# New step lengths and weights for the plan that orders a fused attention and feed-forward kernel

## The chip, the core and the metric

The kernel runs on one core of a Trainium2 chip. The core has a matrix engine (TensorE, in the profile PE for products and PEld for its weight loads), three engines for elementwise work (VectorE as DVE, ScalarE as ACT, GpSimd as POOL) and SyncE (SP), whose queue issues all transfers here. Each engine takes its own instructions in the order in which they were built; engines wait for one another through semaphores. PSUM is the memory into which TensorE writes; SBUF is the working memory.

The metric is the device time of one execution in microseconds (us), as the median of several runs. The profile is of one further execution.

## The reference, cut to what matters

```python
def mab(q, kv):
    s = scale * (q @ kv.transpose(0, 2, 1))
    s = s - s.max(-1, keepdims=True)
    a = np.exp(s)
    a /= a.sum(-1, keepdims=True) + 1e-09
    return a @ kv
h = mab(I, x)          # 32 inducing points attend to 12480 tokens of 128 numbers, 4 batches
attn = mab(x, h)       # every token attends to the 32 results

h = attn.reshape(-1, 128) @ w_in      # 128 x 2048
r = np.maximum(h, 0.0)
g = s * (r * r) + b
out = g @ w_out                       # 2048 x 128
```

All of it is float32, for 49920 tokens.

## The kernel before

**Tiles.** The tokens go in blocks of 480 (BLK), 26 to a batch, 104 in all. The hidden size of 2048 is cut into 16 columns of 128, taken two at a time: a *pair* k is two such columns for one block, a tile of 128 partitions x 2 x 480. There are 8 pairs to a block and 832 in all. `pair(k)` (L813) makes one of them.

**A pair.** PE multiplies the block's attention weights with a matrix in which the attention's result and w_in are joined (L824, two products, into one of three PSUM buffers h). Then r = relu(h) goes to SBUF, by ACT (L840) or by DVE (L842), as the plan chooses. ACT squares r into g1 (`square`, L901), rounded to the narrower float fp32r; where two pairs of the same r tile are ready together, one instruction squares both (960 or 1920 columns). DVE forms the exact square relu(h) x r (L860), and the difference of that and g1, the low part g2, is formed at L878. PE then adds into the block's output bank x: g1 with the low and high parts of w_out, four products, and g2 with the high part, two products (`out_part`, L926). When a block is full, ACT (or DVE) scales it and adds the bias (L934, L936), and SP stores it.

**Two kinds of pair.** In a pair of kind P, DVE writes relu(h) x r to one of four SBUF buffers g, which frees the PSUM buffer h, and POOL subtracts. In a pair of kind D, DVE writes it in place into h and subtracts it itself; h stays taken until then. In the trace, L860 with g<-h,r is a P and L860 with h<-h,r is a D; L878 is on POOL or on DVE. The first 8 pairs (NATIVE) do without a low part, with one product of full float32 for each column.

**Beside the pairs** run the units of the attention: `attend` (L702 to L733) makes a block group's attention weights; `scores`, `top`, `values` and `points` (L614 to L689) prepare the next batch's 32 results, and `w_unit` (L564) the joined matrix. Each block's output bank alternates with one for these units. The first 60 us or so are an opening with the first batch's attention and the splitting of the weights.

**What sets the order.** Nothing on the chip chooses: the class Plan (L76) runs while the kernel is built, and records each instruction when its step is picked. A step is what a generator yields: an engine (or a choice of two) with a length in us, and events that must come first. Plan keeps a clock for each engine, and picks in turn the step that can start earliest, weighted by its urgency:

```python
at, eng = min(((max(ready, self.free.get(e, 0.0)), e) for e in engs),
              key=lambda x: x[0] + engs[x[1]] + lean.get(x[1], 0.0))
able.setdefault(eng, []).append((at + WEIGHT * urgency, at, engs[eng], u))
```

So the lengths decide where a step with a choice goes and who is first on an engine. LAT is the time that an event takes to be seen, SLIP how far another step may push the picked one back, LEAN and R_LEAN what is added for an engine where there is a choice (R_LEAN for r alone). M_U, R_U, S_U, C_U, SQ, OUT and OUT_HI are added to k as the urgency of the product, r, DVE's square, the in-place subtraction, ACT's square and the two output parts. MM is the length of one product. A pair becomes a P where POOL's planned backlog, `pool_work`, is under POOL_Q and a g buffer is free:

```python
wait = max(0.0, pool_work[0] - plan.end)
kind = "P" if wait < POOL_Q and next_free("g", 4) <= plan.start else "D"
```

The lengths and the constants work on the order alone: no instruction waits for a time on the chip.

Of the kernel before, what the change touches and what calls it, by code (L numbers as in the profile page):

```python
# [19 lines left out]
P = 128  # L20
# [5 lines left out]
TB = BLK // 32  # L26
TH = 8
WC = 512

POOL_Q = 4.228  # L30


LAT = 0.180
SLIP = 0.159
WEIGHT = 0.0272
LEAN = {"ACT": -0.50}
R_LEAN = {"DVE": 0.00}


M_U = -5.604  # L40
R_U = 2.437
SQ = 3.369
MM = 0.2165
S_U = -1.313
C_U = -5.000
OUT_HI = 1.632
OUT = 1.982
FRONT = 0.379
FIRST = -200.0
SPREAD = -50.0  # L50
# [3 lines left out]
NATIVE = 8  # L54
# [21 lines left out]
class Plan:  # L76
# [13 lines left out]
    def _step(self, unit, urgency, ready=None):  # L90
        want = next(unit, None)
        if ready is None:
            ready = self.end + LAT
        if want is not None:
            eng, us, *waits = want
            if not isinstance(eng, dict):
                engs, lean = {eng: us}, LEAN
            elif isinstance(us, dict):
# [20 lines left out]
    def run(self):  # L119
        ev = self.events  # L120
        while self.units:
            able = {}
            for u in self.units:
                _, urgency, ready, engs, waits, _, lean = u
                if any(w not in ev for w in waits):
                    continue
                ready = max([ready] + [ev[w] + LAT for w in waits])
                at, eng = min(
# [6 lines left out]
            for eng, steps in able.items():  # L135
                best = min(steps, key=lambda x: x[0])

                fill = [x for x in steps if x[1] + x[2] <= best[1] + SLIP]
                picks.append((*min(fill or [best], key=lambda x: x[0])[1:], eng))
# [8 lines left out]
def tile_attn_relu2(ctx: ExitStack, tc: tile.TileContext, xT, xN, indT, w_in, w_out, s_rep, b_rep, outT):  # L148
# [10 lines left out]
    plan = Plan()  # L159
# [71 lines left out]
    def blocks_in(g):  # L231
        return min(GR, NBLK - g * GR)
# [256 lines left out]
    def h_unit(b, ps, *waits):  # L489
# [17 lines left out]
        nc.vector.reduce_sum(out=l, in_=lw, axis=AX.X)  # L507
        plan.spawn(h_sums(b, l, lambda: ps), FIRST, plan.end + LAT)
        yield "DVE", 0.35
# [45 lines left out]
    def w_unit(b, ps, *waits):  # L555
# [19 lines left out]
        for c in range(nc_):  # L575
            plan.spawn(spread_w(b, c, hl, n, left), SPREAD + c, plan.end + LAT)

# [16 lines left out]
    def scores(b, g, ps, *waits):  # L594
        nb = blocks_in(g)
        rows = M * nb
        if g == 0:
            yield "DVE", 0.15, *waits
            d = st[b] = {
                "mx": sm.tile([P, NG], F32, name="mx"),  # L600
                "l": sm.tile([P, NG], F32, name="l"),
                "s": p1.tile([P, NG, BLK], F32, name="s"),
                "acc": sm.tile([P, P], F32, name="accb", bufs=1),
            }
            last = M * blocks_in(NG - 1)
            if last < P:
                nc.vector.memset(d["mx"][last:P, NG - 1:NG], -3.0e38)
                nc.vector.memset(d["l"][last:P, NG - 1:NG], 0.0)
        d = st[b]
        yield "PE", 0.4 + 0.23 * nb, ("x", b, g, 1), *waits  # L610
        ps = ps()
        xt, turn = xt_tiles[b, g, 1]
        for q in range(nb):
            nc.tensor.matmul(ps[M * q:M * (q + 1), 0:BLK], ind_sb, xt[:, q], start=True, stop=True)  # L614
        plan.set(("xt", turn))
        yield "DVE", 0.65
        nc.vector.reduce_max(out=d["mx"][0:rows, g:g + 1], in_=ps[0:rows, 0:BLK], axis=AX.X)
        yield dict(ACT=0.56, DVE=0.65), 0.0
        copy(d["s"][0:rows, g], ps[0:rows, 0:BLK])
        plan.set(("scores", b, g))  # L620
# [14 lines left out]
    def values(b, g, ps, *waits):  # L635
        d = st[b]
        rows = M * blocks_in(g)
        e = d["s"][0:rows, g]
        yield "ACT", 0.8, ("top", b), *waits
        nc.scalar.activation(  # L640
            out=e, in_=e, func=AF.Exp, bias=d["nm"][0:rows], scale=scale, accum_out=d["l"][0:rows, g:g + 1]
        )
        e_turn, e_free = ring_in_order("eT", 3)
        yield "DVE", 0.66, *e_free
        eT = sm.tile([P, TB, M], F32, name="eT", bufs=3)
        plan.set(("eT", "got", e_turn))
        nc.vector.transpose(out=eT[0:rows].rearrange("p n i -> p (n i)"), in_=e)  # L647
        yield "PE", 1.25, *[("xn", b, g, half) for half in range(-(-TB // TH))]
        ps = ps()
        for n in range(TB):  # L650
            c, half = n % (P // M), n // TH
            nc.tensor.matmul(  # L652
                ps[M * c:M * (c + 1), 0:P], eT[0:rows, n], xn_tiles[b, g, half][0][0:rows, n - half * TH],
                start=n < P // M, stop=n + P // M >= TB,
            )
        for half in range(-(-TB // TH)):
            plan.set(xn_tiles.pop((b, g, half))[1])
        plan.set(("eT", e_turn))
        yield "DVE", 0.29
        if g == 0:  # L660
            nc.vector.tensor_copy(out=d["acc"], in_=ps[:, 0:P])
        else:
            nc.vector.tensor_tensor(out=d["acc"], in0=ps[:, 0:P], in1=d["acc"], op=ALU.add)
        plan.set(("p1", b, g))
# [29 lines left out]
    def attend(b, g, ps, *waits):  # L694
        nb = blocks_in(g)
        rows = M * nb
        yield "PE", 0.4 + 0.23 * nb, ("hT", b), ("x", b, g, 2), *waits
        ps = ps()
        hT = st[b]["hT"]
        xt, turn = xt_tiles[b, g, 2]  # L700
        for q in range(nb):
            nc.tensor.matmul(ps[M * q:M * (q + 1), 0:BLK], hT[:, 0:M], xt[:, q], start=True, stop=True)  # L702
        plan.set(("xt", turn))
        s = ps[0:rows, 0:BLK]
        v = s.rearrange("p (n i) -> p n i", i=M)
        sums = ps[0:rows, BLK:BLK + TB]
        yield "DVE", 0.65
        nc.vector.transpose(out=s, in_=s)  # L708
        yield "DVE", 0.65
        mx = sm.tile([P, TB], F32, name="mx2")[0:rows]  # L710
        nc.vector.reduce_max(out=mx, in_=v, axis=AX.X)  # L711
        yield "DVE", 0.66
        nc.vector.tensor_tensor(out=v, in0=v, in1=mx.unsqueeze(2).broadcast_to([rows, TB, M]), op=ALU.subtract)
        yield "ACT", 0.55
        nc.scalar.activation(out=v, in_=v, func=AF.Exp, scale=scale)  # L715
        yield "DVE", 0.65
        nc.vector.reduce_sum(out=sums, in_=v, axis=AX.X)  # L717
        yield "DVE", 0.16
        nc.vector.tensor_scalar_add(sums, sums, 1e-9)
        yield "DVE", 0.17  # L720
        l = sm.tile([P, TB], F32, name="l2")[0:rows]
        nc.vector.reciprocal(out=l, in_=sums)
        yield "DVE", 0.66
        nc.vector.tensor_tensor(out=v, in0=v, in1=l.unsqueeze(2).broadcast_to([rows, TB, M]), op=ALU.mult)
        yield "DVE", 0.65
        nc.vector.transpose(out=s, in_=s)  # L726
        n, free = ring_in_order("hl", 2)
        yield dict(ACT=0.56, DVE=0.65), 0.0, *free
        hl = p2.tile([P, 2, WC], F32R, name="hl")[:, :, 0:BLK]
        plan.set(("hl", "got", n))  # L730
        copy(hl[0:rows, 0], s)
        yield "DVE", 0.66
        nc.vector.tensor_tensor(out=hl[0:rows, 1], in0=s, in1=hl[0:rows, 0].bitcast(F32), op=ALU.subtract)  # L733
        plan.set(("hl", b, g))
        mine = [q for q in range(nb) if (b, GR * g + q) not in a2t]
        halves[b, g] = hl, n, list(mine)
        for q in mine:
            plan.spawn(spread(b, g, q), SPREAD, plan.end + LAT)

# [71 lines left out]
    pool_work = [0.0]  # L811

    def pair(k):  # L813

        b, blk, pr = place(k)
# [14 lines left out]
        if n == 0:  # L830
            quad[k] = {"r": ring("r", 2), "g1": ring("g1", 4), "g1_uses": 4, "r_uses": 4, "R": []}
        q = quad[k - n]
        yield dict(ACT=0.855, DVE=1.08), R_LEAN, R_U, q["r"][1]
        if n == 0:
            q["r_t"] = ew.tile([P, 4, BLK], F32, name="r", bufs=2)
        native = k < NATIVE
        half = slice(2 * n, 2 * n + 2)
        r = q["r_t"][:, half, :]
        if plan.eng == "ACT":
            nc.scalar.activation(out=r, in_=hv, func=AF.Relu)  # L840
        else:
            nc.vector.tensor_scalar(out=r, in0=hv, scalar1=0.0, scalar2=None, op0=ALU.max)  # L842
        plan.set(("R", k))
        if native:
            g1_used(q, 2)
            q["r_uses"] -= 1
            kind = "N"
            g_turn, g_free = ring("g", 4)
            yield "DVE", 1.07, S_U, g_free
        else:  # L850
            q["R"].append((n, plan.end))
            if len(q["R"]) == 1:
                plan.spawn(square(k - n), k + SQ, plan.end + LAT)
            yield "DVE", 1.07, S_U
            wait = max(0.0, pool_work[0] - plan.end)
            kind = "P" if wait < POOL_Q and next_free("g", 4) <= plan.start else "D"
            if kind == "P":
                g_turn, _ = ring("g", 4)
        g = hv if kind == "D" else ew.tile([P, 2, BLK], F32, name="g", bufs=4)
# [9 lines left out]
            plan.spawn(out_part(k, ops, 1.6, "w_out", lambda: plan.set(("g", g_turn))), k + OUT, plan.end + LAT)  # L869
            return  # L870
        if kind == "P":
            pool_work[0] = max(pool_work[0], plan.end) + 2.17
        n2, free2 = ring("g2", 8)
        yield ("Pool", 2.17, ("Q", k), free2) if kind == "P" else ("DVE", 1.07, C_U, ("Q", k), free2)
        hi = q["g1_t"][:, half, :]
        g2 = ew.tile([P, 2, BLK], F32R, name="g2", bufs=8)
        eng = nc.gpsimd if kind == "P" else nc.vector
# [227 lines left out]
```

## Time and profile before

| | |
|---|---|
| median of 3 runs | 1641.07 us (1640.85 to 1641.46) |
| profiled execution, its own time | 1639.56 us |
| its span, first to last instruction | 1637.8 us |
| granted TensorE clock, mean | 0.997 |
| HBM read, written | 73.52 MB, 25.56 MB |
| transfers' share of 16 DMA engines | 24.3% |

The profile counts an engine as busy while one of its instructions runs. A group's row has its line, engine, operation, tiles (written <- read), shape and count, then busy time and mean ns of one, then the engine's idle time just before them and what ended most of it. Rows of a stretch have, for each engine in the order PE, PEld, DVE, ACT, POOL, busy time and (in brackets) instructions, then the granted clock, the DMA share and GB/s. Rows of the timeline have start, duration, engine, line, operation, tiles and count. Rows of waits have who waited for whom, with total us, times and the longest.

### The profile page before, as it was taken

Reading aid. Unit: us, or ns where it says so; the run is one execution under the profiler, and the core shown is the slowest. Engines: PE = TensorE matmul, PEld = TensorE weight load, DVE = VectorE, ACT = ScalarE, POOL = GpSimd, SP = SyncE. Lnnn points to the kernel's source line nnn. Section 1 sums busy time; section 2 is a strip of 40 time slices with the busy share of each in tenths; the row PEclk is TensorE's granted clock in tenths of the full one; section 3 lists DMA queues with packets and bytes.
Section 4 is the critical chain, followed back from the end, with each engine's and each line's share of the span. In section 5 each row is a group of like instructions: output and inputs, shape, how many; then the busy total and the mean of one; then the engine's idle time right before and its main releaser. Section 6 shows DMA issues by size and latency. Waiting matters only on the chain. (4 is left out here: it accounts for less than half of the span.)

```text
span 1637.8 us, 24676 instructions
## 1 busy us (share of the span) xinstructions
PE 1606.7 (98%) x8147; PEld 1288.9 (79%) x8147; DVE 1454.3 (89%) x1569; ACT 1500.6 (92%) x1755; POOL 1575.8 (96%) x718
## 2 busy tenths in 40 slices
PE   8899999999999999999999999999999999999998
PEld 6577788887887778887778777788778878888887
DVE  6989898989998889888988889989999899998996
ACT  7699999999998899998999999999989999999997
POOL 1499999999999999999999999999999999999998
PEclk9999999999999999999999999999999999999999
DMA  7332222312123222231222322322222112112110
GB/s 261 100 101 97 80 78 97 109 49 87 46 94 115 83 81 87 77 115 55 70 65 97 106 76 73 115 79 85 68 61 67 37 49 67 31 50 66 52 33 20
DMA packets 53982, 130.20 MB, mean 79 GB/s; under 512 B 11488, under 2 KB 37984, under 8 KB 53856
## 3 DMA queue, kind: packets, MB, share of 16 engines
q1 hardware_dynamic: 53856, 128.63, 24.3%
q8 instruction: 66, 1.08, 0.3%
q14 instruction: 60, 0.49, 0.1%
HBM read 73.52 MB, written 25.56 MB: 60 GB/s over the span
## 5 line engine op out<-in xcount | busy, mean ns | idle before, releaser
L878 POOL TENSOR_TENSOR g<-g,g 128x960 fp32r<-128x960 f32 x699 | 1558.8, 2533 | 13.9 <-DVE g L860 13.9
L926 PE MATMUL x<-g,w_hi 128*128 128x480 f32 x3296 | 1046.5, 382 | 5.1 <-POOL g L878 4.6
L860 DVE SCALAR_TENSOR_TENSOR g<-h,r 128x960 f32<-128x960 f32 x707 | 801.8, 1149 | 116.2 <-POOL g L878 61.3
L901 ACT ACTIVATE g<-r 128x960 fp32r<-128x960 f32 x808 | 797.8, 1020 | 40.1 <-DVE r L842 25.0
L926 PEld LDWEIGHTS x<-g,w_hi 128*128 128x128 f32 x3296 | 612.4, 188 | 131.5 <-POOL g L878 27.3
L840 ACT ACTIVATE r<-h 128x960 f32<-128x960 f32 x653 | 619.9, 967 | 56.4 <-PE h L824 49.4
L926 PE MATMUL x<-g,w_lo 128*128 128x480 f32 x1648 | 626.3, 380 | 0.0
L824 PE MATMUL h<-a2t,wst 128*128 128x480 f32 x1664 | 510.8, 388 | 11.2 <-DVE g L860 7.2
L824 PEld LDWEIGHTS h<-a2t,wst 128*128 128x128 f32 x1664 | 302.8, 189 | 105.8 <-issue 32.6
L926 PEld LDWEIGHTS x<-g,w_lo 128*128 128x128 f32 x1648 | 309.3, 188 | 51.7 <-issue 3.4
L842 DVE TENSOR_SCALAR r<-h 128x960 f32<-128x960 f32 x179 | 205.5, 1149 | 16.5 <-PE h L824 15.1
L878 DVE TENSOR_TENSOR g<-h,g 128x960 fp32r<-128x960 f32 x125 | 143.8, 1150 | 6.7 <-ACT g L901 1.4
L860 DVE SCALAR_TENSOR_TENSOR h<-h,r 128x960 f32<-128x960 f32 x125 | 144.6, 1157 | 2.6 <-ACT r L840 1.9
L934 ACT ACTIVATE ob<-x,bias,s_sb 128x480 f32<-128x480 f32 x103 | 77.1, 749 | 9.2 <-PE x L926 8.9
L316 POOL TENSOR_TENSOR w_in_sb<-w_in_sb,g 128x512 f32<-128x512 f32 x4 | 5.2, 1310 | 31.6 <-DVE g L311 31.6
L702 PE MATMUL x<-xt,hT 128*32 128x480 f32 x208 | 29.1, 594 | 0.0
L652 PE MATMUL x<-xn,eT 128*32 128x128 f32 (+1 forms) x630 | 22.5, 275 | 1.7 <-DVE eT L647 1.7
L652 PEld LDWEIGHTS x<-xn,eT 128*32 128x32 f32 (+1 forms) x630 | 16.9, 109 | 8.9 <-DVE eT L647 6.2
L733 DVE TENSOR_TENSOR hl<-x,hl 128x480 fp32r<-128x480 f32 (+1 forms) x28 | 18.2, 650 | 4.9 <-ACT hl L179 4.4
L614 PE MATMUL x<-xt,ind_sb 128*32 128x480 f32 x156 | 21.2, 578 | 0.0
L726 DVE STREAM_TRANSPOSE x<-x 128x480 f32<-128x480 f32 (+1 forms) x28 | 19.5, 697 | 1.0
L717 DVE TENSOR_REDUCE x<-x 128x15 f32<-128x480 f32 (+1 forms) x28 | 18.4, 656 | 2.2 <-ACT x L715 2.0
(151 smaller groups left out, 409.0 us busy)
## 6 DMA issues: line engine op xcount, KB each, us to landing
xt<-in_xT_dram SPq DMA_DIRECT2D x41, 960.0 KB, 5.2
out_dram<-ob SPq DMA_DIRECT2D x104, 240.0 KB, 2.0
a2t<-hl SPq DMA_DIRECT2D x412, 60.0 KB, 2.0
xn<-in_xN_dram SPq DMA_DIRECT2D x18, 512.0 KB, 3.6
xn<-in_xN_dram SPq DMA_DIRECT2D x18, 448.0 KB, 4.3
xt<-in_xT_dram SPq DMA_DIRECT2D x13, 480.0 KB, 4.1
wst<-hl SPq DMA_DIRECT2D x64, 64.0 KB, 2.0
r<-in_xT_dram SPq DMA_DIRECT2D x7, 480.0 KB, 9.0
```

The source lines that it names most:

```text
L614: nc.tensor.matmul(ps[M * q:M * (q + 1), 0:BLK], ind_sb, xt[:, q], start=True, stop=True)
L652: nc.tensor.matmul(ps[M * c:M * (c + 1), 0:P], eT[0:rows, n], xn_tiles[b, g, half][0][0:rows, n - half * TH], start=n < P // M, stop=n + P ...
L702: nc.tensor.matmul(ps[M * q:M * (q + 1), 0:BLK], hT[:, 0:M], xt[:, q], start=True, stop=True)
L726: nc.vector.transpose(out=s, in_=s)
L824: nc.tensor.matmul(h[:, u, 0:BLK], wst[:, c * P:(c + 1) * P], A, start=True, stop=True)
L840: nc.scalar.activation(out=r, in_=hv, func=AF.Relu)
L842: nc.vector.tensor_scalar(out=r, in0=hv, scalar1=0.0, scalar2=None, op0=ALU.max)
L860: nc.vector.scalar_tensor_tensor(out=g, in0=hv, scalar=0.0, in1=r, op0=ALU.max, op1=ALU.mult)
L878: eng.tensor_tensor(out=g2, in0=g, in1=hi.bitcast(F32), op=ALU.subtract)
L901: nc.scalar.activation(out=q["g1_t"][:, sl, :], in_=q["r_t"][:, sl, :], func=AF.Square)
L926: nc.tensor.matmul(o, w, g, start=first and n == 0, stop=left == 0 and n == len(ops) - 1)
L934: nc.scalar.activation(out=ob, in_=o, func=AF.Identity, bias=bias, scale=s_sb)
```

## The change

Only numbers change. Step lengths of the plan: a subtraction on POOL 2.17 to 2.237, DVE's steps of a pair 1.07 or 1.08 to 1.065, a product 0.2165 to 0.2174, LAT 0.180 to 0.1855, and the products of `scores`, `attend` and `values`. Weights: the constants below. A line that sets `native` moves down by some lines, which alters nothing but the line numbers between (L840 and L842 become L839 and L841).

```diff
-POOL_Q = 4.228
+POOL_Q = 3.0602
...
-LAT = 0.180
-SLIP = 0.159
+LAT = 0.1855
+SLIP = 0.179
 WEIGHT = 0.0272
-LEAN = {"ACT": -0.50}
-R_LEAN = {"DVE": 0.00}
+LEAN = {"ACT": -0.622}
+R_LEAN = {"DVE": -0.222, "ACT": 0.024}
...
-M_U = -5.604
-R_U = 2.437
-SQ = 3.369
-MM = 0.2165
+M_U = -6.0646
+R_U = 1.7476
+SQ = 3.3894
+MM = 0.2174
 S_U = -1.313
-C_U = -5.000
-OUT_HI = 1.632
-OUT = 1.982
+C_U = -5.0529
+OUT_HI = 2.3715
+OUT = 1.9651
...
-        yield "PE", 0.4 + 0.23 * nb, ("x", b, g, 1), *waits
+        yield "PE", 0.45 + 0.22 * nb, ("x", b, g, 1), *waits
...
-        yield "PE", 1.25, *[("xn", b, g, half) for half in range(-(-TB // TH))]
+        yield "PE", 1.3, *[("xn", b, g, half) for half in range(-(-TB // TH))]
...
-        yield dict(ACT=0.855, DVE=1.08), R_LEAN, R_U, q["r"][1]
+        yield dict(ACT=0.855, DVE=1.065), R_LEAN, R_U, q["r"][1]
...
-            yield "DVE", 1.07, S_U
+            yield "DVE", 1.065, S_U
...
-            pool_work[0] = max(pool_work[0], plan.end) + 2.17
+            pool_work[0] = max(pool_work[0], plan.end) + 2.237
         n2, free2 = ring("g2", 8)
-        yield ("Pool", 2.17, ("Q", k), free2) if kind == "P" else ("DVE", 1.07, C_U, ("Q", k), free2)
+        yield ("Pool", 2.237, ("Q", k), free2) if kind == "P" else ("DVE", 1.065, C_U, ("Q", k), free2)
```

What the new numbers do to the order is seen in the built kernels. Over the whole program, what changes in number:

| step | engine | before | after |
|---|---|---|---|
| subtraction of a P pair (L878) | POOL | 699 | 673 |
| subtraction of a D pair (L878) | DVE | 125 | 151 |
| r = relu(h) | DVE | 179 | 217 |
| r = relu(h) | ACT | 653 | 615 |
| square of one pair (L901) | ACT | 792 | 674 |
| square of two pairs (L901) | ACT | 16 | 75 |

The 824 pairs that are not among the first 8 are P or D: 699 and 125 before, 673 and 151 now. Products on PE and transfers are the same in number.

The first place is DVE in the middle of the program, just behind the fourth batch's first `scores` step on DVE. Numbers behind a name are those of its buffers. Before, there stand:

```order
L842 TENSOR_SCALAR r_8722<-h_8714 128x960
L860 SCALAR_TENSOR_TENSOR g_8730<-h_8703,r_8690 128x960
L860 SCALAR_TENSOR_TENSOR g_8740<-h_8714,r_8722 128x960
L860 SCALAR_TENSOR_TENSOR h_8725<-h_8725,r_8722 128x2x480
L860 SCALAR_TENSOR_TENSOR g_8761<-h_8743,r_8750 128x960
L878 TENSOR_TENSOR g2_8773<-h_8725,g1_8734 128x960
L860 SCALAR_TENSOR_TENSOR g_8783<-h_8758,r_8750 128x960
L860 SCALAR_TENSOR_TENSOR g_8802<-h_8785,r_8792 128x960
L860 SCALAR_TENSOR_TENSOR h_8794<-h_8794,r_8792 128x2x480
L842 TENSOR_SCALAR r_8825<-h_8804 128x960
L878 TENSOR_TENSOR g2_8834<-h_8794,g1_8809 128x960
```

And now, at the same place:

```order
L841 TENSOR_SCALAR r_8676<-h_8673 128x960
L860 SCALAR_TENSOR_TENSOR g_8687<-h_8663,r_8676 128x960
L860 SCALAR_TENSOR_TENSOR h_8673<-h_8673,r_8676 128x2x480
L860 SCALAR_TENSOR_TENSOR g_8708<-h_8684,r_8699 128x960
L878 TENSOR_TENSOR g2_8719<-h_8673,g1_8691 128x960
L860 SCALAR_TENSOR_TENSOR g_8727<-h_8702,r_8699 128x960
L841 TENSOR_SCALAR r_8740<-h_8729 128x960
L860 SCALAR_TENSOR_TENSOR g_8747<-h_8729,r_8740 128x960
L860 SCALAR_TENSOR_TENSOR h_8737<-h_8737,r_8740 128x2x480
L860 SCALAR_TENSOR_TENSOR g_8771<-h_8749,r_8763 128x960
L841 TENSOR_SCALAR r_8763<-h_8765 128x960
L878 TENSOR_TENSOR g2_8789<-h_8737,g1_8752 128x960
```

In both there are five P and two D with their subtractions; of the relus r, three now stand in DVE's row where two stood.

The second place is DVE in the opening, from the sixth of the first 8 pairs on. Before:

```order
L860 SCALAR_TENSOR_TENSOR g_767<-h_754,r_745 128x960
L333 TENSOR_REDUCE w_sum_93<-wst_109 128x128
L860 SCALAR_TENSOR_TENSOR g_786<-h_769,r_774 128x960
L344 TENSOR_SCALAR bias_94<-x1_86,b_sb_89 128x1
L860 SCALAR_TENSOR_TENSOR g_796<-h_777,r_774 128x960
L860 SCALAR_TENSOR_TENSOR h_790<-h_790,r_798 128x2x480
L878 TENSOR_TENSOR g2_809<-h_790,g1_800 128x960
L860 SCALAR_TENSOR_TENSOR g_812<-h_803,r_798 128x960
```

And now:

```order
L860 SCALAR_TENSOR_TENSOR g_766<-h_753,r_744 128x960
L333 TENSOR_REDUCE w_sum_93<-wst_109 128x128
L860 SCALAR_TENSOR_TENSOR g_786<-h_768,r_773 128x960
L860 SCALAR_TENSOR_TENSOR g_789<-h_776,r_773 128x960
L333 TENSOR_REDUCE w_sum_93<-wst_109 128x128
L860 SCALAR_TENSOR_TENSOR g_805<-h_791,r_796 128x960
```

In both the first three g rows are the last of the 8; then a D stood ahead of the first P (g_812), and now the first P (g_805) comes at once, behind the second sum over w_out, which stood further up before.

The third place is the end of PE's row, the output products of the last pairs (g2 is a low part, g1 a rounded square; x2 means two products). Before:

```order
L926 MATMUL x1_86<-g2_15944,w_hi_91 128x480 x2
L926 MATMUL x1_86<-g1_15930,w_lo_92 128x480
L926 MATMUL x1_86<-g1_15930,w_hi_91 128x480
L926 MATMUL x1_86<-g1_15930,w_lo_92 128x480
L926 MATMUL x1_86<-g1_15930,w_hi_91 128x480
L926 MATMUL x1_86<-g1_15930,w_lo_92 128x480
L926 MATMUL x1_86<-g1_15930,w_hi_91 128x480
L926 MATMUL x1_86<-g1_15930,w_lo_92 128x480
L926 MATMUL x1_86<-g1_15930,w_hi_91 128x480
L926 MATMUL x1_86<-g2_15961,w_hi_91 128x480 x2
L926 MATMUL x1_86<-g2_15973,w_hi_91 128x480 x2
```

And now:

```order
L926 MATMUL x1_86<-g2_15867,w_hi_91 128x480 x2
L926 MATMUL x1_86<-g2_15876,w_hi_91 128x480 x2
L926 MATMUL x1_86<-g1_15860,w_lo_92 128x480
L926 MATMUL x1_86<-g1_15860,w_hi_91 128x480
L926 MATMUL x1_86<-g1_15860,w_lo_92 128x480
L926 MATMUL x1_86<-g1_15860,w_hi_91 128x480
L926 MATMUL x1_86<-g2_15882,w_hi_91 128x480 x2
```

Before, the low parts of the last two pairs, both from POOL, stood at the end; now the last but one is a D, its low part (g2_15876) comes from DVE, and four products stand ahead of POOL's last (g2_15882).

More of the change, by code (lines that the diff above doesn't have):

```diff
@@ L696, in attend @@
         rows = M * nb
-        yield "PE", 0.4 + 0.23 * nb, ("hT", b), ("x", b, g, 2), *waits
+        yield "PE", 0.45 + 0.22 * nb, ("hT", b), ("x", b, g, 2), *waits
         ps = ps()
@@ L832, in pair @@
         q = quad[k - n]
-        yield dict(ACT=0.855, DVE=1.08), R_LEAN, R_U, q["r"][1]
+        yield dict(ACT=0.855, DVE=1.065), R_LEAN, R_U, q["r"][1]
         if n == 0:
             q["r_t"] = ew.tile([P, 4, BLK], F32, name="r", bufs=2)
-        native = k < NATIVE
         half = slice(2 * n, 2 * n + 2)
@@ L843, in pair @@
         plan.set(("R", k))
+        native = k < NATIVE
         if native:
@@ L848, in pair @@
             g_turn, g_free = ring("g", 4)
-            yield "DVE", 1.07, S_U, g_free
+            yield "DVE", 1.065, S_U, g_free
         else:
```

## The prediction

> **What bounds the kernel now.** I read the page's first part, then the groups by line, then POOL's timeline at its first and last steps, then the waits.
>
> ```profile
> PE 1606.7 (98%) x8147; PEld 1288.9 (79%) x8147; DVE 1454.3 (89%) x1569; ACT 1500.6 (92%) x1755; POOL 1575.8 (96%) x718
> ```
>
> Four engines stand at 89% to 98%, so the page alone does not name the bound. The next rows do: first the stretch from POOL's first subtraction to the end of the work, then POOL's group, its first run, and the last two rows of PE and ACT.
>
> ```profile
> 74.50:1634.00 1559.50, 1542.66 (x7624) 1247.63 (x7622) 1395.77 (x1462) 1452.29 (x1677) 1558.77 (x699) 1.00 0.23 74
> ...
> L878 POOL TENSOR_TENSOR g<-g,g 128x960 fp32r<-128x960 f32 x699 | 1558.8, 2533 | 13.9 <-DVE g L860 13.9
> ...
> 74.52 35.72 POOL L878 TENSOR_TENSOR g<-g,g 128x960 fp32r<-128x960 f32 x16 [13.89 <-DVE g L860]
> ...
> 1633.34 0.71 PE L926 MATMUL x<-g,w_hi 128*128 128x480 f32 x2 [1.13 <-POOL g L878]
> 1634.08 0.75 ACT L934 ACTIVATE ob<-x,bias,s_sb 128x480 f32<-128x480 f32 x1 [6.92 <-PE x L926]
> ```
>
> The reader is to see that POOL is busy 1558.77 of 1559.50 us, and that its 699 subtractions waited once only, 13.9 us before the first. So a subtraction takes 1558.8 / 699 = 2.230 us of POOL (the mean of 2533 ns counts overlapping records), and the span is a sum with one long term: 74.5 until the first + 699 x 2.230 = 1558.8 + 4.5 from the last one's end (1633.3) over the last products, the result and its store = 1637.8. From 74.5 us on POOL alone sets the end. The plan of before counted 2.17 for this step; against 2.230 that is 699 x 0.06 = 42 us too little, and an order that hands POOL so many steps makes the other engines wait for it.
>
> PE is the runner-up, and here the 98% misleads, because a product's record runs on while the next one streams. The piece of the chain quoted first below has 18 products in 3.89 us, 0.2161 each; I take 0.217, since it is one of the chain's longest pieces without a pause. Per pair of tiles there are 8 products, 8 pairs at the beginning have 2 of this kind: 824 x 8 + 16 = 6608 products.
>
> ```profile
> 1587.24 3.89 PE x L926 x18
> ...
> 53.30 2.18 PE L824 MATMUL h<-a2t,wst 128*128 128x480 f32 x6
> ...
> L926 PE MATMUL x<-g,wst 128*128 128x480 f32 x32 | 15.2, 602 | 0.0
> ...
> L702 PE MATMUL x<-xt,hT 128*32 128x480 f32 x208 | 29.1, 594 | 0.0
> L652 PE MATMUL x<-xn,eT 128*32 128x128 f32 (+1 forms) x630 | 22.5, 275 | 1.7 <-DVE eT L647 1.7
> ...
> L614 PE MATMUL x<-xt,ind_sb 128*32 128x480 f32 x156 | 21.2, 578 | 0.0
> ...
> L564 PE MATMUL x<-w_in_sb,hT 128*32 128x512 f32 x24 | 3.2, 605 | 0.0
> ```
>
> PE's work from its first product at 53.3 to the last at 1634.0 is 6608 x 0.217 = 1433.9, plus 15.2, 29.1, 22.5, 21.2 and 3.2 = 1525.1 us, of 1580.7. So PE stands still for 55.6 us in all, and with none of that the span would be 1582.2. Who makes PE wait is in the waits:
>
> ```profile
> DVE g L860 <- POOL g L878: 61.3, 105, 1.1
> ...
> DVE g L860 <- ACT r L840: 44.1, 70, 1.7
> ...
> PEld x L926 <- POOL g L878: 27.3, 60, 1.5
> ...
> PEld h L824 <- DVE g L860: 20.2, 31, 3.3
> ...
> DVE r L842 <- PE h L824: 15.1, 26, 1.8
> ...
> PE h L824 <- DVE g L860: 7.2, 12, 2.9
> ```
>
> PE's products (or the weight loads ahead of them, PEld) wait for POOL directly, 27.3 us, and for DVE, 20.2 + 7.2 = 27.4; and DVE itself waits longest for POOL, 61.3 us, because POOL has not given back one of the four g buffers.
>
> **The change part by part.** The built order of the changed kernel has the same arithmetic on PE, and these other counts: POOL subtractions 699 to 673; in-place pairs on DVE, which need a second DVE step, 125 to 151; relu steps r on DVE 179 to 217 and on ACT 653 to 615; squares of two pairs at once on ACT 16 to 75, of one pair 792 to 674.
>
> POOL: 26 steps fewer are 26 x 2.230 = 58.0 us. Its line becomes 74.5 + 673 x 2.230 + 4.5 = 1579.8.
>
> DVE: 26 subtractions and 38 relus more. The price of one more step in a row is the second row below less the mean of the first, 2.21 - 1.149 = 1.061 us.
>
> ```profile
> L860 DVE SCALAR_TENSOR_TENSOR g<-h,r 128x960 f32<-128x960 f32 x707 | 801.8, 1149 | 116.2 <-POOL g L878 61.3
> ...
> 874.07 2.21 DVE L860 SCALAR_TENSOR_TENSOR g<-h,r 128x960 f32<-128x960 f32 x2
> ```
>
> 64 x 1.061 = 67.9, so DVE's busy time goes from 1454.3 to 1522.2. What hides it is DVE's own idle time of 1637.8 - 1454.3 = 183.5 us, of which 61.3 were waits for POOL. If that cover is gone, the price is the whole of the third rival.
>
> ACT: 38 relus fewer and 59 times one square in place of two.
>
> ```profile
> L840 ACT ACTIVATE r<-h 128x960 f32<-128x960 f32 x653 | 619.9, 967 | 56.4 <-PE h L824 49.4
> ...
> L901 ACT ACTIVATE g<-r 128x1920 fp32r<-128x1920 f32 x16 | 29.0, 1810 | 0.3
> ...
> 848.69 1.90 ACT L901 ACTIVATE g<-r 128x960 fp32r<-128x960 f32 x2
> ```
>
> That is 38 x 619.9 / 653 = 36.1 and 59 x (1.90 - 1.81) = 5.3 less, 1459 us busy. A double square hands its first pair to PE about 0.9 us later; of this the trace of before shows no cost (0.3 us of idle before 16 of them). Bounds: nothing, and 59 x 0.9 = 53 if PE stood still each time; I take nothing, as eight buffers of subtracted tiles and the other pairs' products stand between, and keep a part of the upper end in the range.
>
> An in-place pair keeps its PSUM buffer h, one of three, until the second DVE step, and PE's next h product queues behind that; behind a waiting product stand all other products, since PE takes them in order. Bounds of the 26 new ones: nothing, and the longest such wait above, 3.3 us each = 86. The nearest rows are PE's two waits on DVE: 27.4 us for 125 in-place pairs, 0.22 each even if every one of those waits came from them; so 6 us by that, and the part that fits enters the sum below.
>
> The beginning: in before the ninth pair was an in-place one, now it goes to POOL. Two DVE steps (2.1 us) no longer stand ahead of POOL's first subtraction, but a sum over w_out (L333) that stood earlier on now stands there. I take nothing; bounds 2.1 us either way. The end: PE's last two pairs are no longer both POOL's, worth at most the 1.13 us in the row of 1633.34. The transfers move with their steps in SP's queue; DMA is 0.23 busy in the row of 74.5 to 1634 and no wait of PE on a transfer stands among those of that stretch, so nothing for them either, or at most one issue pause; the same holds for the re-ordered small units of the beginning.
>
> Now the sum. Both floors are close, POOL 1579.8 and PE 1582.2, so PE's is next. Of its 55.6 us of standing still, POOL's direct share goes: 27.3 of 54.7 is half, 27.8 us. Of the 27.8 that DVE caused, the part in which DVE itself waited for POOL goes too: 61.3 of the three largest waits of DVE (61.3 + 44.1 + 15.1 = 120.5), 51%, which leaves 13.6. DVE holds PE more often with 151 in-place pairs than with 125: 13.6 x 1.21 = 16.5. Span 1582.2 + 16.5 = 1598.7. The profiled execution took 1639.56, 1.8 over its span; the median of the three runs, 1641.07, is 1.5 over that. So 1598.7 + 1.8 + 1.5 = 1602.0 us, 2.4% below before; POOL then has some 19 us of gaps (1598.7 - 1579.8).
>
> A rule that speaks against PE as the next limit: the Trainium skill, "Perfetto Trace Analysis", section "Identifying the Most-Contended Engine", says that matmul busy time does not tell how near TensorE is to its limit, and that the busy share of weight loads (with the achieved FLOP rate) does. By that, 79% leaves PE a fifth of the span, and POOL's floor alone would count. The first half agrees with this trace (98% busy, yet 55.6 us free); the second does not, since the 18 products in 3.89 us follow one another without a pause, while the weight loads are busy for 79% of the span. It is the first rival.
>
> **The rivals.** *PE gives way and POOL stays the bound.* POOL never runs dry: 1579.8 + 3.3 = 1583. For it: POOL did not run dry once in 699 steps. Against: PE would have to lose all of its 55.6 us of standing still, while products wait in order for three engines. Chance 0.13.
>
> *Half a relief.* What DVE does to PE is its own in-order queue and not POOL's lag: then 27.8 x 1.21 = 33.6 stay, 1582.2 + 33.6 + 3.3 = 1619. For it: 44.1 us of waiting for ACT's r. Against: the 105 waits for POOL come first. It reaches on to about 1636 when the 59 double squares cost PE some 0.3 us each. Chance 0.13.
>
> *DVE becomes the bound (slower).* DVE has 122.2 us of idle time that does not end with POOL (183.5 - 61.3). If all of it stays, because it waits in its fixed order for ACT and PE, DVE's line is 1522.2 + 122.2 = 1644.4, + 3.3 = 1648. It decides from 115.6 us of such idle time on, since 1637.8 - 1522.2 = 115.6. Against: waits for ACT's r and PE's h shrink where these are themselves held by POOL. Chance 0.05.
>
> *The change doesn't do what it says.* The new order fits no better, and POOL gets gaps of 58 us, 0.086 a step: about 1641. Against: its step lengths (1.065 on DVE, 2.237 on POOL) lie within 0.01 of the 1.061 and 2.230 above. Chance 0.02.
>
> **How the numbers follow.** The forecast, from 1588 to 1617, has the remaining 0.67. The range takes in POOL's floor with 1 us of gain at the beginning, 1582, and half a relief with a little of the double squares' upper end, 1621; outside stay the far part of half a relief (0.07), the last two rivals (0.07) and a few hundredths at the low end. All but the last two rivals are faster by over 0.2% (3.3 us, about what a measurement of this kernel can tell from no change): faster 0.93, same 0.02, slower 0.05.
>
> **What would show it.** Right: POOL's 673 steps at 2.23 us each again, but now with waits on DVE's g or ACT's squares between them, about 19 us; DVE's wait for POOL well under 61.3; PE standing still for about 17 us in place of 55.6. Wrong: POOL without gaps and a span near 1580 (first rival); waits of PE for DVE's h over 30 us (second); DVE busy over 95% with its waits for r unchanged (third); a POOL step of another length would upset the first term itself.

## The result, and the profile after

The changed kernel takes **1612.42 us** (median of 4 runs, 1611.61 to 1612.73) against 1640.96 (1640.61 to 1641.46): a ratio of 0.9825, with a 95% interval of 0.9808 to 0.9842. That is 28.5 us less. Forecast were 1602.0 us, with a range of 1582 to 1621; the time lies in the range, and the gain is three quarters of the 39 us forecast.

The page's first part for the changed kernel, the stretch from POOL's first subtraction to the end of the products (columns as before: PE, PEld, DVE, ACT, POOL), and POOL's group:

```profile
PE 1594.4 (99%) x8147; PEld 1294.3 (80%) x8147; DVE 1512.5 (94%) x1629; ACT 1455.0 (90%) x1662; POOL 1522.4 (95%) x692
...
77.16:1606.00 1528.84, 1528.02 (x7623) 1252.27 (x7621) 1456.58 (x1527) 1406.86 (x1582) 1504.60 (x673) 1.00 0.24 76
...
L878 POOL TENSOR_TENSOR g<-g,g 128x960 fp32r<-128x960 f32 x673 | 1504.7, 2299 | 38.8 <-ACT g L901 15.9
```

PE and POOL have changed places. PE's records have 0.8 us of gaps in 1528.84; POOL, which had none before, now stands still for 1528.84 - 1504.60 = 24.2 us, and its waits are for squares of ACT (15.9 us) and for DVE. The waits of the same kernel:

```profile
ACT r L839 <- PE h L824: 69.8, 98, 3.0
...
POOL g L878 <- ACT g L901: 15.9, 24, 1.3
POOL g L878 <- DVE bias L344: 14.6, 1, 14.6
PEld h L824 <- DVE g L860: 14.0, 21, 4.6
DVE g L860 <- ACT r L839: 12.9, 40, 1.1
...
PE h L824 <- DVE g L860: 4.5, 2, 4.2
...
DVE g L860 <- POOL g L878: 2.8, 3, 1.2
...
PEld x L926 <- POOL g L878: 1.9, 5, 0.8
```

DVE's wait for POOL fell from 61.3 to 2.8 us and PE's from 27.3 to 1.9, so the old bound is gone from the list. What has grown is waiting *for PE*: ACT's relus now wait 69.8 us for a product (49.4 before). The chain that ended last says the same: it covers the whole span, and PE has 96% of it. (The chain of before reaches back over only 36% of its span, with 21% on PE and 7% on POOL, so the two shares can't be set side by side.)

### The profile page after: what moved, and what is told of

Read it like the earlier page. It is cut to its first block, busy times and chain, and to the rows that moved or that the text cites. A ratio compares the mean times of both kernels' runs of the same rounds, so it can differ in the third digit from the quotient of the medians.

```text
span 1610.6 us, 24689 instructions
## 1 busy us (share of the span) xinstructions
PE 1594.4 (99%) x8147; PEld 1294.3 (80%) x8147; DVE 1512.5 (94%) x1629; ACT 1455.0 (90%) x1662; POOL 1522.4 (95%) x692
## 3 DMA queue, kind: packets, MB, share of 16 engines
q8 instruction: 66, 1.08, 0.3%
## 4 chain that ended last, share of the span: by engine, by line
PE 96%; DVE 2%; ACT 1%; issue 1%; DMA 0%; POOL 0%; POOLq 0%; DVEq 0%; ACTq 0%
PE x L926 67%; PE h L824 23%; PE x L702 2%; PE x L652 1%; PE x L614 1%; PE h L408 1%; DVE g L860 0%; ACT r L839 0%; PE x L433 0%; DVE g L311 0%; ACT g L901 0%; DMA xt<-in_xT_dram 0%; DVE wst L309 0%; PE x L564 0%; PE x L462 0%
## 5 line engine op out<-in xcount | busy, mean ns | idle before, releaser
L878 POOL TENSOR_TENSOR g<-g,g 128x960 fp32r<-128x960 f32 x673 | 1504.7, 2299 | 38.8 <-ACT g L901 15.9
L926 PE MATMUL x<-g,w_hi 128*128 128x480 f32 x3296 | 1076.3, 380 | 0.1
L901 ACT ACTIVATE g<-r 128x960 fp32r<-128x960 f32 (+1 forms) x749 | 795.5, 1089 | 35.1 <-PE x L926 17.9
L860 DVE SCALAR_TENSOR_TENSOR g<-h,r 128x960 f32<-128x960 f32 x681 | 768.0, 1148 | 23.2 <-ACT r L839 12.9
L839 ACT ACTIVATE r<-h 128x960 f32<-128x960 f32 x615 | 591.9, 970 | 75.8 <-PE h L824 69.8
L841 DVE TENSOR_SCALAR r<-h 128x960 f32<-128x960 f32 x217 | 249.8, 1153 | 27.3 <-PE h L824 24.7
L860 DVE SCALAR_TENSOR_TENSOR h<-h,r 128x960 f32<-128x960 f32 x151 | 174.5, 1157 | 4.4 <-ACT r L839 4.1
L878 DVE TENSOR_TENSOR g<-h,g 128x960 fp32r<-128x960 f32 x151 | 173.5, 1150 | 4.4 <-ACT g L901 0.8
L652 PE MATMUL x<-xn,eT 128*32 128x128 f32 (+1 forms) x630 | 22.6, 275 | 0.0
L614 PE MATMUL x<-xt,ind_sb 128*32 128x480 f32 x156 | 21.2, 578 | 0.0
L726 DVE STREAM_TRANSPOSE x<-x 128x480 f32<-128x480 f32 (+1 forms) x28 | 19.5, 697 | 0.9
L708 DVE STREAM_TRANSPOSE x<-x 128x480 f32<-128x480 f32 (+1 forms) x28 | 19.2, 687 | 0.6 <-PE x L702 0.6
```

Source lines behind the costliest of these rows:

```text
L652: nc.tensor.matmul(ps[M * c:M * (c + 1), 0:P], eT[0:rows, n], xn_tiles[b, g, half][0][0:rows, n - half * TH], start=n < P // M, stop=n + P ...
L860: nc.vector.scalar_tensor_tensor(out=g, in0=hv, scalar=0.0, in1=r, op0=ALU.max, op1=ALU.mult)
L878: eng.tensor_tensor(out=g2, in0=g, in1=hi.bitcast(F32), op=ALU.subtract)
L901: nc.scalar.activation(out=q["g1_t"][:, sl, :], in_=q["r_t"][:, sl, :], func=AF.Square)
L926: nc.tensor.matmul(o, w, g, start=first and n == 0, stop=left == 0 and n == len(ops) - 1)
```

## The experiments

All but the last are single runs with a profile. Beside the first four the kernel before took 1639.64 us on the same chip, beside the next four 1638.18, and beside the last three 1639.99 (median of 9). So differences of 1 to 2 us between single runs of different groups say little.

**One length alone, and the change without it.** Of all the numbers, the theory needs one: POOL's step, 2.17 us in the plan and 2.230 in the trace. The first kernel is that of before with this edit and no other:

```diff
-            pool_work[0] = max(pool_work[0], plan.end) + 2.17
+            pool_work[0] = max(pool_work[0], plan.end) + 2.237
-        yield ("Pool", 2.17, ("Q", k), free2) if kind == "P" else ...
+        yield ("Pool", 2.237, ("Q", k), free2) if kind == "P" else ...
```

> The kernel before with one part of the change alone: the plan counts 2.237 us instead of 2.17 for a subtraction on POOL. Its order has 680 subtractions on POOL (before 699, after 673) and 169 relus on DVE. Theory (POOL's undercounted step made POOL the only bound): most of the gain comes with it, POOL's line is 74.5 + 680 x 2.230 + 4.5 = 1595 and PE's next, so POOL gets gaps and the time is 1610 to 1622. Rival (the weights bring the gain, the length only shifts a few steps): 1630 to 1641, POOL still without gaps.

The second is the changed kernel with these lines as they were before:

> The changed kernel with that one part undone: 2.17 us again for a subtraction on POOL, all other lengths and weights new. Its order has 695 subtractions on POOL. Theory: POOL is full again, without gaps, and sets the end at 77.2 + 695 x 2.230 + 4.5 = 1631.6, so 1633 to 1635. Rival (the weights bring the gain): 1612 to 1618, POOL with gaps.

The third has the changed kernel's weights (POOL_Q, SLIP, LEAN, R_LEAN, M_U, R_U, SQ, C_U, OUT_HI, OUT) with all old lengths, the fourth all new lengths (POOL, DVE, MM, LAT, the units' products) with the old weights:

> All new weights with all old lengths (692 subtractions on POOL). Theory: POOL without gaps again, 77.2 + 692 x 2.230 + 4.5 = 1625, so 1625 to 1628. Rival (the weights bring the gain): under 1618.

> All new lengths with all old weights (683 subtractions on POOL). Theory: POOL's line is 74.5 + 683 x 2.230 + 4.5 = 1602, below PE's, so the time is 1612 to 1622 with gaps on POOL; what is over 1612 is what the new weights are worth. Rival (the weights bring the gain): over 1630.

| kernel | POOL steps | time, us | span, us |
|---|---|---|---|
| before, beside these | 699 | 1639.64 | |
| POOL's length alone | 680 | 1609.30 | 1607.4 |
| all lengths alone | 683 | 1611.30 | 1609.5 |
| weights alone | 692 | 1634.94 | 1633.2 |
| the change without POOL's length | 695 | 1634.30 | 1632.4 |
| the change | 673 | 1612.42 | 1610.6 |

The one length brings 30.3 us, no less than the whole change; without it the change brings 5.3, and the weights alone 4.7. So the weights did not bring the gain. POOL's groups in the second, the third and the first kernel:

```profile
L878 POOL TENSOR_TENSOR g<-g,g 128x960 fp32r<-128x960 f32 x695 | 1550.6, 2333 | 15.0 <-DVE bias L344 14.5
```

```profile
L878 POOL TENSOR_TENSOR g<-g,g 128x960 fp32r<-128x960 f32 x692 | 1544.1, 2314 | 21.3 <-DVE bias L344 13.6
```

```profile
L878 POOL TENSOR_TENSOR g<-g,g 128x960 fp32r<-128x960 f32 x680 | 1519.1, 2290 | 22.6 <-DVE g L860 20.4
```

With POOL's old length back, POOL waited 15.0 us, 14.5 of them before its first step, and ended as 695 x 2.23 us in a row after 76.8: the expectation of 1633 to 1635 held (1634.3). The weights alone were expected at 1625 to 1628 and took 1634.9: there POOL had 21.3 - 13.6 = 7.7 us of gaps besides, which the expectation left out. The other two came 0.7 us under their ranges: 1609.3 for 1610 to 1622, and 1611.3 for 1612 to 1622.

**Less work on PE.** If PE is the bound now, and was not before, taking products away must show in the one and not in the other. Both kernels now leave 103 products with the low part of w_out out of the result:

```diff
-            ops = [... for u in range(2) for w in (w_lo, w_hi)]
+            ops = [... for u in range(2) for w in ((w_lo, w_hi) if u == 0 or pr != NPAIR - 1 else (w_hi,))]
```

> The changed kernel in the same order, but 103 products fewer on PE: in the last pair of each block but the first, the rounded square of the second column isn't multiplied with the low part of w_out (left out of the result). The plan still counts its time, so nothing else moves. Theory (PE is the bound now, almost without gaps): 103 x 0.2174 = 22.4 us go, and since POOL's line is 77.2 + 673 x 2.230 + 4.5 = 1582.5, most of it shows: 1590 to 1598 against 1612. Rival (the fixed order of DVE and ACT sets the end): 1608 to 1612.

> The same 103 products left out in the kernel before, in its own order. Theory (POOL alone was its bound): no change, 1639 to 1641, with POOL again without gaps. Rival (PE was a bound of before too): 1618 to 1630.

The kernel before took 1640.24 us, no less than the 1638.18 beside it. Its stretch of steady work shows why; PE stands still for 25 us and POOL is full:

```profile
74.50:1590.00 1515.50, 1490.50 (x7336) 1190.23 (x7336) 1362.55 (x1433) 1417.81 (x1639) 1513.95 (x680) 1.00 0.23 75
```

(POOL's missing 1.55 us lie before its first step at 76.05.) So POOL alone was the bound of before: shown. The changed kernel took 1601.23 us, 11.2 less (some 8 by the ratios to the kernel before beside each), where 14 to 22 were expected and 0 to 4 by the rival: both missed. Half or more of the 22.4 us came back as waits, as these rows of it show:

```profile
PEld h L824 <- DVE g L860: 18.1, 26, 5.6
...
PEld x L926 <- POOL g L878: 10.5, 24, 1.0
```

Against the changed kernel's 14.0 and 1.9 us these are 12.7 more. The starts of the products say it more directly: from 77.2 to 1590 us, steps of over 0.24 us from one product to the next hold 16.8 us beyond the usual step here and 5.5 in the changed kernel, 11.3 more. PE is the bound of the changed kernel, but not by much: with 1.4% less work it runs into POOL and DVE again.

**The opening.** The changed kernel is 3.1 us slower than the one with POOL's length alone, and its POOL starts later. This one keeps the old constants (weights, LAT and MM) up to the eighth pair; the lengths that stand in the steps are the new ones throughout:

```diff
     def pair(k):
+        if k == 8:
+            globals().update(NEW)
```

> The changed kernel with the order of before up to the eighth pair: the plan uses the old constants until it comes to the ninth pair and the new ones from there. Theory (the new numbers cost 2 to 3 us in the opening, where POOL's first subtraction came at 77.2 in place of 74.5): 1609 to 1610. Rival (the 3 us against the kernel with POOL's length alone were lost among the later pairs): 1612.

It took 1610.69 us, between the two and outside the theory's 1609 to 1610 as well as the rival's 1612. The 1.7 us against the changed kernel are no more than single runs differ by; the traces say more, see *The opening* in the next section. What happens there is seen in DVE's timeline, first of before, then of the changed kernel:

```profile
53.76 0.42 DVE L302 TENSOR_SCALAR g<-g 128x512 int32<-128x512 int32 x1
...
55.99 0.69 DVE L311 SCALAR_TENSOR_TENSOR g<-g,g 128x512 int32<-128x512 int32 x1
...
57.16 1.15 DVE L860 SCALAR_TENSOR_TENSOR g<-h,r 128x960 f32<-128x960 f32 x1
```

```profile
53.56 1.51 DVE L302 TENSOR_SCALAR g<-g 128x512 int32<-128x512 int32 x1
...
56.89 1.75 DVE L311 SCALAR_TENSOR_TENSOR g<-g,g 128x512 int32<-128x512 int32 x1
...
59.13 1.14 DVE L860 SCALAR_TENSOR_TENSOR g<-h,r 128x960 f32<-128x960 f32 x1
...
74.00 1.95 DVE L333 TENSOR_REDUCE w_sum<-wst 128x128 f32<-128x1024 f32 x1
75.86 1.15 DVE L860 SCALAR_TENSOR_TENSOR g<-h,r 128x960 f32<-128x960 f32 x1
```

The first pair's step on DVE starts at 59.13 us, where before it started at 57.16. The same steps of weight preparation stand ahead of it in both, but L302 and L311 took 1.51 and 1.75 us in place of 0.42 and 0.69. POOL is busy for 5.87 of the 7 us from 53 to 60 here and for 2.45 before; that this is the reason is not shown. Later, the second sum over w_out (L333) stands right ahead of the step that feeds POOL's first subtraction, which comes at 77.16 in place of 74.52.

**More than the measured length.** The kernel before with 2.30 and with 2.45 us for POOL's step, and the changed one with 2.30:

> The kernel before with 2.30 us for POOL's step, more than the measured 2.23 (662 subtractions on POOL, 162 in-place pairs). Theory (PE is the bound once POOL is not overfilled): no worse than the right length by more than a few us, 1607 to 1615, with POOL gaps of some 55 us. Rival (every pair taken from POOL beyond need costs DVE and PE's h buffers): 1618 or more.

> The kernel before with 2.45 us for POOL's step (626 subtractions on POOL, 198 in-place pairs). Theory (PE's own work is the floor, and DVE has room): flat, 1606 to 1614, POOL with gaps of some 130 us. Rival (in-place pairs hold PE's h buffers): 1620 or more, with PE's waits for DVE over 30 us.

> The changed kernel with 2.30 us for POOL's step (656 subtractions on POOL, 168 in-place pairs). Theory (PE's work is the floor of every such order, the weights neither help nor harm beyond some 3 us): 1607 to 1613. Rival (the new weights with more DVE work overfill DVE): over 1615.

| POOL's length in the plan | other numbers | POOL steps | time, us | POOL's idle time before its steps, us |
|---|---|---|---|---|
| 2.17 | before | 699 | 1639.64 | 13.9 |
| 2.237 | before | 680 | 1609.30 | 22.6 |
| 2.30 | before | 662 | 1607.69 | 58.3 |
| 2.45 | before | 626 | 1620.79 | 149.3 |
| 2.237 | changed | 673 | 1612.42 | 38.8 |
| 2.30 | changed | 656 | 1615.41 | 79.5 |

With the old weights the step is steep on one side: 0.06 us too little costs 30 us, 0.07 too much costs nothing, and only 0.22 too much costs 12 or so. At 2.45 the theory (1606 to 1614) missed and the rival had the time (1620.8, over its 1620), but not by the wait it named: PE's weight loads waited 17.6 us for DVE and PE itself 5.9, not over 30. PE stands still again there: its records have 4.4 us of gaps from 77.2 to 1600 us, and none with 2.30. At 2.30 with the new weights the theory (1607 to 1613) missed too, and the time lies at the rival's edge (1615.4, over its 1615), 3 us worse than with 2.237; the runs do not say why.

The fastest, 2.30 with the old weights, was timed again:

> The kernel of the run with 2.30 us for POOL's step again, timed in five rounds, since it was the fastest so far. If its single time holds: 1607 to 1609, a ratio to before of about 0.980.

It took 1608.26 us (1607.48 to 1609.37, 5 runs), a ratio of 0.9804 to before (0.9791 to 0.9818). So two edited lines of the kernel before do at least as well as the whole change. Its slowest run is 2.2 us under the changed kernel's fastest, but the two were not timed beside each other and their intervals overlap, so that it is the faster of the two is not shown.

## Why the prediction held, and where its size was off

*POOL alone set the end of before.* Right, and shown from both sides: less work on PE changed nothing, and the order with POOL's old length filled POOL again.

*POOL's price and its new line.* Right: 673 steps took 1504.7 / 673 = 2.236 us each, gaps of 24.2 us where 19 were forecast. "POOL stays the bound" fell.

*DVE and ACT.* DVE's 1512.5 us of busy time were forecast as 1522.2, ACT's 1455.0 as 1459. That DVE's idle time apart from POOL would stay, the slower rival, fell: its wait for ACT's r went from 44.1 to 12.9 us. But the reason that the forecast gave, that such waits are POOL's lag at second hand, is refuted. First the kernel with POOL's length alone, where DVE's wait for POOL is down to 4.5 us; then the change without it, where POOL is full:

```profile
DVE g L860 <- ACT r L840: 60.8, 99, 2.7
```

```profile
DVE g L860 <- ACT r L839: 20.7, 46, 1.4
```

Relieving POOL alone made this wait longer, and the weights made it shorter. It cost no time that could be seen: the kernel with 60.8 us of it took 1609.30.

*PE's waits.* Forecast were 16.5 us, from a sum that took the listed waits of PE and its weight loads (54.7 us before) for PE's standing still (55.6). In the list the changed kernel has 14.0 + 4.5 us for DVE and 1.9 for POOL, not far off. But the waiting of a weight load is not PE's standing still, because an earlier product can be running meanwhile. The kernel with 2.30 us for POOL's step shows it. In its stretch from 74.50 to 1590 us PE's records have no gap at all, and yet the list of that stretch has

```profile
PEld h L824 <- DVE g L860: 7.6, 15, 0.8
...
PEld x L926 <- POOL g L878: 4.0, 5, 0.8
```

What PE lost is read better from the starts of its products. From one product to the next it is mostly 0.218 us; the steps of over 0.24 us, from 77.2 to 1590 us and not counting those next to a unit, hold beyond that 29.4 us in the kernel before, 5.5 in the changed one and 4.5 in the one without a gap. In the changed kernel one wait in the opening comes on top:

```profile
60.33 1.17 PE L824 MATMUL h<-a2t,wst 128*128 128x480 f32 x2 [4.16 <-DVE g L860]
```

That is some 10 us, not 16.5, and some 32 before (2.9 in the opening), not 55.6. The factor of 1.21 for more in-place pairs has no support: the kernel without a gap has 162 of them, the changed one 151.

*The step that failed is PE's floor*, "6608 x 0.217 = 1433.9, plus 15.2, 29.1, 22.5, 21.2 and 3.2 = 1525.1 us", and with it "PE stands still for 55.6 us in all". Between the first and the last product of the changed kernel lie:

```profile
53.76 2.41 PE L824 MATMUL h<-a2t,wst 128*128 128x480 f32 x6
...
1605.67 1.16 PE L926 MATMUL x<-g,w_hi 128*128 128x480 f32 x3
```

That is 1606.8 - 53.8 = 1553.0 us, 27.9 over the floor, with only some 10 us of waits. How far the floor was off is seen where PE has no gap, in the kernel with 2.30 us for POOL's step:

```profile
74.50:1590.00 1515.50, 1515.50 (x7568) 1244.31 (x7567) 1399.36 (x1473) 1452.13 (x1687) 1471.09 (x658) 1.00 0.24 76
...
L926 PE MATMUL x<-g,w_hi 128*128 128x480 f32 x3261 | 1033.4, 381 | 0.0
L926 PE MATMUL x<-g,w_lo 128*128 128x480 f32 x1634 | 621.5, 380 | 0.0
L824 PE MATMUL h<-a2t,wst 128*128 128x480 f32 x1636 | 499.0, 386 | 0.0
```

By the forecast's prices these 6531 products are 6531 x 0.217 = 1417.2 us, and the busy times of the other groups in its sum are 76.9 in this stretch: 1494.1. PE needed 1515.5, 21.4 us more, and only 4.5 of them were late starts. So the floor was some 17 us too low: of the 55.6 us in which PE was to stand still before, that much was work.

Where the 17 us lie is seen in rows and in the starts of the products, though no run tested the parts one by one. A product's spacing is not 0.217: one of the longest pieces of PE in the chain of the changed kernel has 3.92 / 18 = 0.2178 us,

```profile
495.69 3.92 PE x L926 x18
```

and the usual step in the starts of the stretch above is 0.2178 too, which makes 5.2 us for 6531. A switch back from a unit costs besides:

```profile
473.43 1.01 PE L614 MATMUL x<-xt,ind_sb 128*32 128x480 f32 x8
474.37 0.70 PE L824 MATMUL h<-a2t,wst 128*128 128x480 f32 x2
474.92 0.38 PE L926 MATMUL x<-g,w_lo 128*128 128x480 f32 x1
```

Two products after a unit take 474.92 - 474.37 = 0.55 us and not 0.435. In the starts of the kernel without a gap the second product comes 0.32 us after the first at 84 places, which makes another 8.7 us. Four small groups of the units (L478, L486, L674, L684; 3.9 us of busy time) were not in the sum at all. The three make 17.8 us; they overlap a little.

So the forecast had two errors of opposite sign, and that its span came within 11.9 us (1598.7 for 1610.6) is in part luck: some 17 us too little work, and 16.5 - 10 = 6.5 too much waiting. These two make 10.5 of the 11.9 us, the later first product (53.76 for 53.30) 0.5; the rest stays open. The time is 10.4 us off, since the 1.5 us that were added for the median did not come.

*The opening* was taken at nothing, with 2.1 us either way. Priced in the same way, the products from 77.2 us on take 22.2 us over their price in the changed kernel, 22.1 with the old constants up to the eighth pair and 22.0 with POOL's length alone. So the 3.2 us between the spans of the first and the last lie almost wholly ahead of 77.2, and the order behind it lost nothing. How much of them is the order's doing stays open: the granted clock from 60 to 77.2 us was 0.83, 0.90 and 0.95 in these three, and 0.12 of 17.2 us is 2 us.

*Double squares cost nothing* was taken as well. The same numbers are in keeping with it: the changed kernel has 75 of them and that with POOL's length alone 11, at 22.2 and 22.0 us over the price.

That PE's floor is a property of the program and not of this order is seen in the other orders. POOL's line by 2.230 us a step lies at 1555 with 662 steps, 1582 with 673, 1596 with 680 and 1604 with 683; the spans are 1605.9, 1610.6, 1607.4 and 1609.5, and the products from 77.2 us on take 21.3, 22.2, 22.0 and 22.6 us over their price. POOL's line moves over 49 us, the span over 5. With still fewer steps or other weights PE gets waits again (1619.0 at 626, 1613.6 at 656).

The rule from "Perfetto Trace Analysis" of the Trainium skill, section "Identifying the Most-Contended Engine", judges PE by its FLOP rate and by the busy share of weight loads. By the second alone, 1244.31 of 1515.50 us leave PE 18% of headroom in the stretch above. This run speaks against that here: PE had no gap and 4.5 us of late starts, POOL had 44 us of gaps, and the time did not follow POOL's line down.

*Half a relief*, the rival at 1619, is nearer in time (6.6 us off, the forecast 10.4), but its reason was not found: PE's waits for DVE were 18.5 us even by the list, not 33.6.

## What to carry to other kernels

Where a planner hands work to several engines by counted lengths, measure each length as the distance between neighbours on a busy engine, and round up that of the engine which is nearest to full: an undercount adds up over all its steps (here 699 x 0.06 us), while 3% too much cost nothing here with the old weights and 10% too much cost 12 us. When a relief is sized, take the next engine's floor from start to start over whole stretches, units and switches included; a product's best spacing times the count gave a floor 17 us too low. Do not add up waits of weight loads as time that PE lost: look at the steps between the starts of its products. And before weights are set anew together with a length, the length should be tried alone: here it had the whole gain.

## What was not expected of the hardware

After a unit of products with 32 columns, the first two products of the usual shape take 0.55 us and not 0.435 (rows of 473.43 to 474.92): the second one starts late, 0.32 us after the first in the mean of 72 such places in the kernel with 2.30 us for POOL's step, and the page's busy times do not show it. POOL's subtraction keeps its length beside a busier DVE: 1558.8 / 699 = 2.230 us with DVE at 89% and 1550.6 / 695 = 2.231 with DVE at 92%.
